# Delta-rule attention with an MoE layer on one core: GpSimd's clamp, sign and scaling in other two-operation forms, all signs on GpSimd, new planner costs and ranks

## The chip, the cores and the metric

One NeuronCore of a Trainium2 chip. The time is device microseconds from start to end of one execution. A run of the kernel before gives 619.16 to 619.97 us.

## The reference

Delta-rule attention over 4 batches, 8 heads, 768 steps, head size 48, and behind it a layer of 384 to 2048 to 384 whose weights come in as 64-bit floats.

```python
def _attn_ref(q, k, v, beta):
    k_n = k / (np.linalg.norm(k, axis=-1, keepdims=True) + 1e-06)
    for t in range(S):
        kt, vt, bt = (k_n[:, :, t], v[:, :, t], beta[:, :, t, None])
        y[:, :, t] = np.einsum('bhd,bhde->bhe', q[:, :, t], state)
        v_old = np.einsum('bhde,bhd->bhe', state, kt)
        state = state + bt[:, :, :, None] * np.einsum('bhd,bhe->bhde', kt, vt - v_old)

def _moe_ref(x, w_in, w_out):          # x: 3072 x 384, from y
    h = x @ w_in
    sp = np.where(h > 20.0, h, np.log1p(np.exp(np.minimum(h, 20.0))))
    return ((h * np.tanh(sp)) @ w_out).astype(np.float32)
```

## The kernel before

**Chunks.** The 768 steps are cut into 12 chunks of 64. Two chunks make a group. `early(g)` does a group's part that needs no state: it loads and transposes the keys (`kt`, L531), multiplies them with themselves (`pg`, L547/L553), masks the products (L562, L567, L576), turns them (L591), and solves a triangular system row by row on VectorE (L673/L674, transposes L687 to L698). For groups 0 and 1 the solve is split in halves, which `merge(n)` joins with two sets of small products, `ma` (L718) and `mb` (L730). Then per chunk come the stages `s_a`, `s_b` (`ta`, `tb`), `s_gq`, `s_z` and `s_y`, all issued from L753; the last one yields the new state and the chunk's 384 x 256 input `x` to the layer (L1080, L1081).

**The layer.** `moe(n)` works on chunk n in eight units. A unit is an up group of 18 matmuls (`h`, L1108), Mish, a cast and a difference (L1124 to L1126), and a down group of 12 matmuls (`acc`, L1118). So the whole kernel has 96 up and 96 down groups.

**The weights.** The 64-bit weights are 28 parts, three `i` parts (128x512) and four `o` parts (128x384) for each quarter of the layer. `convert(k)` turns part k into a pair of 32-bit matrices: ScalarE scales the upper words (L429), a clamp (L443) on GpSimd or VectorE, a sign (L440 on GpSimd, L438 on VectorE), two joins on VectorE (L447) which shift in the lower bits, a negated rounding on ScalarE (L459), and the remainder, on VectorE (L470) for the first 13 parts and over TensorE (L464, L466, L468) from part 13. Clamps are on GpSimd for all parts but part 6; signs are on VectorE for 14 of the 28 parts. Units 0 and 1 of a chunk need quarter 0 of the `i` parts, units 2 and 3 quarter 1, and so on.

**The order.** Nothing runs in program order. Each step is an `op(engine, took, rank, ...)`, and `Plan.run` replays all engines with the durations `took`, takes at each moment the ready step of least rank, and so writes the order of every engine's queue once, when the kernel is built. Ranks are in units of chunks: `moe(n)` has n to n+1 (its differences n + fp/8 + 0.1, its down groups n + (fp + LAG)/8), `convert(k)` has `CV0 + CV1 k/28`, and `early(1)` has `E1 + E1S x`, where x is 0 at the loads of the keys, 0.02 to 0.2 at the transposes, 0.3 to 0.9 in the solve and 0.94 at the merge. Stages of chunk 1 take `c1`, those of later chunks `cc`.

**Loads.** All go through SyncE's queue but some at the start. `EW` is the part from which the loads of weights wait for the group products of chunk 1; `HELD` is a part whose load waits for the first `ma`; `PACE` is how many parts a load may be ahead of the scaling of the parts before it; `KW` picks the weight loads that the first keys and values follow. `BURN` counts tiny matmuls (16x16) between chunk 0's stages. `scale_v` scales a chunk's values by the keys' norms, on ScalarE to chunk 3 and on GpSimd from chunk 4 (L912, eight instructions of 48 columns).

Of the kernel before, what the change touches and what calls it, by code (L numbers as in the profile page):

```python
# [13 lines left out]
ALU = mybir.AluOpType  # L14
# [54 lines left out]
class Plan:  # L69
# [18 lines left out]
    def op(self, engine, took, prio, fn, *after, bufs=(), kb=0, words=0):  # L88
        o = Op(engine, took, prio, fn, after, [b for b in bufs if b is not None])
        o.kb, o.words = kb, words  # L90
        for b in o.bufs:
            b.ops.append(o)
        self.ops.append(o)
        return o
# [127 lines left out]
def kernel(  # L222
# [181 lines left out]
    def convert(k, got, loads):  # L404
        kind, i = parts[k]
        n = 512 if kind == "i" else DM
        u = n / 512.0
        prio = PRIO_CV(k)
        tag = TEMPS[k] if k < len(TEMPS) else ("t0", "t1", "w", "w", "s0", "s1")[(k - len(TEMPS)) % 6]
        if tag in ("t0", "t1"):  # L410
            tmp = Buf(tag, lambda: solved().rearrange("p a b -> p (a b)")[:, 512 * int(tag[1]):512 * int(tag[1]) + 512])
            held = [tmp, solved]
        elif tag in ("s0", "s1"):
            base = spare[int(tag[1])]
            tmp = Buf(tag, lambda: base()[:, 0:512])
            held = [tmp, base]
        else:
            tmp = buf(tag, [P, 512], f"m{kind}{i}")
            held = [tmp]

        def a():
            return tmp()[:, :n]

        def words():
            return raw[kind, i].rearrange("p (a b) -> p a b", b=2)


        def scaled():
            marks[copied[k]] = nc.scalar.activation(a(), words()[:, :, 1].bitcast(F32), AF.Copy, scale=2.0 ** -112).ins  # L429

        copied[k] = o = op("ACT", 0.16 + 0.51 * u, prio, scaled, got, bufs=held)
        if EW < k < len(parts) - PACE:
            loads[k + PACE].after.append(o)

        def sign(engine):
            s = words()[:, :, 1].bitcast(F32)
            if engine == "DVE":
                nc.vector.tensor_scalar(words()[:, :, 1], words()[:, :, 1], -2 ** 31, None, op0=ALU.bitwise_and)  # L438
            else:
                nc.gpsimd.tensor_scalar(s, a(), 0.0, None, op0=ALU.mult)  # L440

        def clamp(engine):
            engine.tensor_scalar(a(), a(), -F64_MOST * 2.0 ** -112, F64_MOST * 2.0 ** -112, op0=ALU.max, op1=ALU.min)  # L443

        def join(x, n, f):
            ai = a().bitcast(I32)
            return nc.vector.scalar_tensor_tensor(ai, *((ai, n, x) if f == ALU.logical_shift_left else (x, n, ai)), op0=f, op1=ALU.bitwise_or).ins  # L447

        o = op("POOL", 0.25 + 1.72 * u, prio, lambda: clamp(nc.gpsimd), o, bufs=held) if k in CLAMP_POOL else \
            op("DVE", 0.14 + 0.39 * u, prio, lambda: clamp(nc.vector), o, bufs=held)  # L450

        e = "DVE" if k in SIGN_DVE else "POOL"
        o = op(e, 0.13 + 0.38 * u if e == "DVE" else 0.43 + 1.12 * u, prio, lambda: sign(e), o, bufs=held)
        o = op("DVE", 0.06 + 0.8 * u, prio, lambda: join(words()[:, :, 1], 3, ALU.logical_shift_left), o, bufs=held)
        o = op("DVE", 0.06 + 0.8 * u, prio, lambda: join(words()[:, :, 0], 29, ALU.logical_shift_right), o, bufs=held)

        def first():
            w = wt[kind, i] = cp.tile([P, 2, n], F32R, tag=f"w{kind}{i}", name=f"w{kind}{i}")
            nc.scalar.mul(out=w[:, 0], in_=a(), mul=-1.0)  # L459

        hi = op("ACT", 0.16 + 0.47 * u, prio, first, o, bufs=held)
        if k in LO_PE:
            ps = buf(f"acc{k % 2}" if k < 6 else "ps", [P, 512], f"lo{kind}{i}")
            p1 = op("PE", 0.05 + 0.5 * u, prio, lambda: nc.tensor.matmul(ps()[:, :n], ident, a(), start=True, stop=False),  # L464
                    o, eyer, bufs=[*held, ps], words=4)
            p2 = op("PE", 0.03 + 0.22 * u, prio, lambda: nc.tensor.matmul(  # L466
                ps()[:, :n], identr, wt[kind, i][:, 0], start=False, stop=True), p1, hi, bufs=[ps], words=2)
            return op("ACT", 0.12 + 0.48 * u, prio, lambda: nc.scalar.mul(  # L468
                out=wt[kind, i][:, 1], in_=ps()[:, :n], mul=-1.0), p2, bufs=[ps])
        return op("DVE", 0.1 + 0.58 * u, prio, lambda: nc.vector.scalar_tensor_tensor(  # L470
            wt[kind, i][:, 1], a(), -1.0, wt[kind, i][:, 0], op0=ALU.mult, op1=ALU.subtract), hi, bufs=held)
# [50 lines left out]
    def early(g, at, gate=None):  # L522
# [3 lines left out]
        for t2 in range(2):  # L526
# [45 lines left out]
            if g:  # L572

                def first_block(hh, t2=t2, am=am):
                    r = slice(64 * hh, 64 * hh + 32)
                    nc.gpsimd.affine_select(out=dt()[r, t2], in_=am()[r], pattern=[[0, NP], [1, 32]], compare_op=ALU.is_ge, fill=0.0,  # L576
                                            base=0, channel_multiplier=-1)

                last = last_s["at", n]
                outs += [op("POOL", 1.37, at(0.17 + 0.03 * t2), lambda hh=hh, f=first_block: f(hh), last, *outs[-2:], made, bufs=[am, dt])  # L580
                         for hh in range(2)]
                last_s["first", n] = outs[-2:]
        gr = buf("gt", [P, 33, 32], f"gt{g}")
# [67 lines left out]

        if g < ROOTS:
            o = op("DVE", 0.38, at(0.25), norms, o, last_s.get("root"), bufs=[gr])
            o = op("ACT", 1.7 if g else 0.25, at(0.25), guess, o)
            last_s.setdefault("guess", o)
            o = op("DVE", 1.45, at(0.25), root, o)
        else:
            o = op("DVE", 3.9, at(0.25), lambda: (norms(), steps(), root()), o, last_s.get("root"), bufs=[gr])
        o = op("DVE", 0.93 if split else 1.45, at(0.26), scale, o, cut, *(betas if g == 0 else ()), bufs=[gr])
        nes[g] = ne  # L660
        ned[g] = last_s["root"] = op("DVE", 0.25, at(0.27), turned, o, last_s.get("turned"), bufs=[bp, ne])
# [29 lines left out]
        if split:  # L691
            ym = buf(*(("gt", [P, 33, 32]) if g else ("g", [P, 32, 32])), f"ym{g}")
            c = op("POOL", 0.6, at(0.9), lambda: nc.gpsimd.memset(ym()[:, :32, 16:], 0.0), u if g else cleared_rest, bufs=[ym])
            last_s["ym"] = c
            for t2 in range(2):
                merge(2 * g + t2, lambda x, t2=t2: at(0.94 + x) + 0.3 * t2 if g or not t2 else XA - 0.25 + x, u, c, o, dt, tu, ym, tn)
        else:
            tnd[2 * g] = tnd[2 * g + 1] = op("DVE", 2.24, at(0.97), lambda: nc.vector.transpose(  # L698
                tn().rearrange("p a b j -> p j (a b)"), gt().rearrange("p i j -> p j i")), o, bufs=[gr, tn])
            for t2 in range(2):  # L700
                ttd[2 * g + t2] = op("POOL", 1.42, at(0.98), lambda t2=t2: move_diagonal(t2), o)
# [198 lines left out]
    def scale_v(n, h, prio, *after):  # L900
        vt, ne = vts[n, h], nes[n // 2]
        n16 = NP * (n % 2) + PB * h
        if n <= 3:
            def scaled():
                for p in range(PB):
                    nc.scalar.mul(out=vt()[:, p, :], in_=vt()[:, p, :], mul=ne()[:, n16 + p:n16 + p + 1])

            vdn[n, h] = op("ACT", 1.9, prio, scaled, ned[n // 2], *after, bufs=[vt.base, ne])
            return
        def scaled():  # L910
            for p in range(PB):
                nc.gpsimd.tensor_scalar(vt()[:, p, :], vt()[:, p, :], ne()[:, n16 + p:n16 + p + 1], None, op0=ALU.mult)  # L912

        vdn[n, h] = op("POOL", 3.4, prio, scaled, ned[n // 2], *after, bufs=[vt.base, ne])

    def turn_q(n, h, prio, got):
        def turn():
# [219 lines left out]
                   bufs=[o], kb=0.3)  # L1137


    SOON, SOON1, E1, EG, ES, LATE1, LATE = -0.099, 2.914, 0.577, -0.653, 1.745, 0.496, 0.249  # L1140
    E1S, LAG, PRIO_XT, CV0, CV1, G1A, XA, GQ2 = 0.074, 3.993, 0, -0.2, 0.877, 1.076, 0.45, 1.157
    LO_PE = range(13, 28)
    HELD, MASKS, ROOTS = 5, 1, 2
    plan.MARGIN = 1
    KW, EW, BURN, TQ, PACE = 2, 0, 84, 2, 4
    plan.TOGETHER = 0.003
    CLAMP_POOL = [k for k in range(len(parts)) if k < 6 or k >= 7 and k % 4 < 4]
    SIGN_DVE = [k for k in range(len(parts)) if k % 4 >= 2]
    TEMPS = ("g", "g", "e", "e", "w", "w", "s0", "s1")

    def PRIO_CV(k):
# [38 lines left out]
    for h in range(2):  # L1190
        issue(0.01 + 0.05 * h, s_y(0, h, y=False))

    cc = [x - SOON for x in (0.05, 0.28, 0.5, 0.72)]
    c1 = [x - SOON1 for x in (0.3, 0.45, 0.68, 0.82)]
    nxt = {1: prep(1, -0.2)}

    def ready(n, h, prio):
# [79 lines left out]
```

## Time and profile before

| | |
|---|---|
| timed runs | 619.16, 619.7 and 619.97 us, median 619.7 |
| span of the profiled execution, its own time | 621.0 us |
| mean granted TensorE clock | 0.956 |
| busy, TensorE matmul / VectorE / ScalarE / GpSimd | 584.7 / 438.9 / 282.0 / 174.3 us |

The profiled execution has no time besides its span, so 1.3 us lie between it and the median of the runs. A share over the whole span mixes two stages: a start, in which weights are converted and the first chunks' states are worked out, and a long stretch in which TensorE has units of the layer to do all the time.

### The profile page before, as it was taken

Reading aid. Unit: us, or ns where it says so; the run is one execution under the profiler, and the core shown is the slowest. Engines: PE = TensorE matmul, PEld = TensorE weight load, DVE = VectorE, ACT = ScalarE, POOL = GpSimd, SP = SyncE. Lnnn points to the kernel's source line nnn. Section 1 sums busy time; section 2 is a strip of 40 time slices with the busy share of each in tenths; the row PEclk is TensorE's granted clock in tenths of the full one; section 3 lists DMA queues with packets and bytes.
Section 4 is the critical chain, followed back from the end, with each engine's and each line's share of the span. In section 5 each row is a group of like instructions: output and inputs, shape, how many; then the busy total and the mean of one; then the engine's idle time right before and its main releaser. Section 6 shows DMA issues by size and latency. Waiting matters only on the chain.

```text
span 621.0 us, 23486 instructions
## 1 busy us (share of the span) xinstructions
PE 584.7 (94%) x10264; PEld 543.1 (87%) x10264; DVE 438.9 (71%) x955; ACT 282.0 (45%) x631; POOL 174.3 (28%) x259
## 2 busy tenths in 40 slices
PE   7657999998899999999999999999999999999997
PEld 4346877897889999999999899999899999999996
DVE  4869899987168999379897579895789893631110
ACT  1838787574344333544324534335433335343321
POOL 6469799211000442013051014131104420000000
PEclk9657899997699999999999999999999999999999
DMA  7958655341025123243114333114041220110001
GB/s 115 225 146 244 150 169 115 54 52 29 4 33 95 18 41 52 29 67 67 30 23 70 42 56 53 33 26 67 17 81 25 41 49 6 29 28 1 6 22 27
DMA packets 156264, 37.81 MB, mean 61 GB/s; under 512 B 149504, under 2 KB 152576, under 8 KB 156160
## 3 DMA queue, kind: packets, MB, share of 16 engines
q1 hardware_dynamic: 151040, 35.80, 29.4%
q8 instruction: 81, 1.33, 1.0%
q10 hardware_dynamic: 5120, 0.49, 0.6%
q14 instruction: 23, 0.19, 0.1%
HBM read 31.56 MB, written 4.72 MB: 58 GB/s over the span
## 4 chain that ended last, share of the span: by engine, by line
PE 78%; POOL 9%; DVE 5%; issue 3%; ACT 2%; DMA 1%; POOLq 0%; DVEq 0%
PE acc L1118 32%; PE h L1108 31%; PE py L753 3%; PE gq L753 3%; PE pz L753 2%; POOL mi L443 2%; PE pg L547 2%; PE ps L753 2%; POOL spare L443 2%; POOL ro L440 1%; POOL solved L443 1%; PE tb L753 1%; POOL ri L440 1%; PE ta L753 1%; PE warm L491 1%
## 5 line engine op out<-in xcount | busy, mean ns | idle before, releaser
L1108 PE MATMUL h<-x,wi 128*128 128x256 f32 x1728 | 226.3, 287 | 1.3 <-issue 0.6
L1118 PE MATMUL acc<-wo,g 128*128 128x384 f32 x1152 | 224.7, 345 | 1.8 <-issue 1.7
L1108 PEld LDWEIGHTS h<-x,wi 128*128 128x128 f32 x1728 | 218.2, 192 | 4.4 <-issue 0.8
L1118 PEld LDWEIGHTS acc<-wo,g 128*128 128x128 f32 x1152 | 201.8, 191 | 7.9 <-issue 4.0
L1126 DVE TENSOR_TENSOR g<-e,g 128x512 fp32r<-128x512 f32 x96 | 69.5, 729 | 93.3 <-ACT g L1125 81.3
L1124 ACT ACTIVATE e<-h 128x512 f32<-128x512 f32 x96 | 57.4, 598 | 126.0 <-PE h L1108 71.6
L1125 ACT CAST g<-e 128x512 fp32r<-128x512 f32 x96 | 59.5, 620 | 65.7 <-PE acc L1118 64.3
L912 POOL TENSOR_SCALAR vt<-vt,ne 128x48 f32<-128x48 f32 x128 | 57.5, 475 | 65.9 <-DMA vt<-in_v_dram 49.3
L674 DVE TENSOR_TENSOR gt<-gt,pr 128x84 f32<-128x84 f32 (+14 forms) x148 | 48.9, 330 | 5.1
L673 DVE TENSOR_TENSOR pr<-gt 128x84 f32<-128x84 f32 (+14 forms) x148 | 47.4, 321 | 3.4
L576 POOL TENSOR_SCALAR_AFFINE_SELECT d<-at 32x512 f32<-32x512 f32 x20 | 14.4, 720 | 101.1 <-ACT at L567 100.3
L777 ACT COPY xx<-pz 64x192 f32<-64x192 f32 x92 | 28.9, 314 | 22.2 <-PE pz L753 20.7
L970 DVE TENSOR_TENSOR xx<-gq,amask 64x256 f32<-64x256 f32 x88 | 37.1, 422 | 1.6
L706 POOL COPY tt<-tt 32x512 f32<-32x512 f32 x24 | 17.4, 725 | 71.3 <-DVE tt L689 49.2
L963 DVE TENSOR_TENSOR vt<-vt,gq 64x192 f32<-64x192 f32 (+1 forms) x66 | 23.3, 353 | 19.0 <-PE gq L753 18.1
L753 PE MATMUL gq<-xx,kt 64*64 64x112 f32 (+1 forms) x768 | 30.6, 264 | 2.5 <-ACT xx L938 2.5
L1067 DVE TENSOR_TENSOR xx<-xx,ps 48x192 f32<-48x192 f32 x80 | 28.2, 352 | 3.2 <-PE ps L753 1.6
L921 DVE STREAM_TRANSPOSE xx<-qsrc 64x512 f32<-64x512 f32 x40 | 28.2, 706 | 1.1
L753 PEld LDWEIGHTS py<-xx 128*32 128x32 f32 (+1 forms) x1536 | 23.5, 111 | 5.7 <-issue 3.6
L753 PE MATMUL py<-xx 128*32 128x64 f32 (+1 forms) x1536 | 27.8, 227 | 0.7 <-ACT xx L777 0.4
L753 PE MATMUL pz<-vt,tt 64*64 64x48 f32 x768 | 27.8, 225 | 0.6 <-ACT tt L777 0.6
L753 PEld LDWEIGHTS pz<-vt,tt 64*64 64x64 f32 x768 | 22.7, 140 | 5.3 <-issue 2.1
(146 smaller groups left out, 611.4 us busy)
## 6 DMA issues: line engine op xcount, KB each, us to landing
ri<-in_moe_w_in_dram SPq DMA_DIRECT2D x12, 512.0 KB, 5.2
ro<-in_moe_w_out_dram SPq DMA_DIRECT2D x16, 384.0 KB, 4.4
vt<-in_v_dram SPq DMA_DIRECT2D x24, 192.0 KB, 4.4
xx<-in_k_dram SPq DMA_DIRECT2D x48, 96.0 KB, 3.1
out_dram<-o SPq DMA_DIRECT2D x48, 96.0 KB, 2.2
ksrc<-in_k_dram SPq DMA_DIRECT2D x44, 64.0 KB, 3.0
qsrc<-in_q_dram SPq DMA_DIRECT2D x40, 64.0 KB, 2.5
ksrc<-in_k_dram SPq DMA_DIRECT2D x44, 32.0 KB, 2.6
```

The costliest lines, as they stand in the source:

```text
L443: engine.tensor_scalar(a(), a(), -F64_MOST * 2.0 ** -112, F64_MOST * 2.0 ** -112, op0=ALU.max, op1=ALU.min)
L673: nc.vector.tensor_tensor(out=pv, in0=nj, in1=xj, op=ALU.mult)
L674: return nc.vector.tensor_tensor(out=below, in0=below, in1=pv, op=ALU.add).ins
L753: last = nc.tensor.matmul(*a, **flags)
L777: (nc.scalar.copy if e == "ACT" else nc.vector.tensor_copy)(out=a, in_=b)
L912: nc.gpsimd.tensor_scalar(vt()[:, p, :], vt()[:, p, :], ne()[:, n16 + p:n16 + p + 1], None, op0=ALU.mult)
L970: nc.vector.tensor_tensor(out=x[r, p4, hh, Q0:K0], in0=pg[h4]()[i, :, d:], in1=bcast_mid(amask[i], 4), op=ALU.mult)
L1108: nc.tensor.matmul(h()[:, f2, :], wt["i", f * P // WI * NCH + c][:, i2, f0:f0 + P], x[:, c, :], start=(i == 0), stop=(i == 3 * NCH - 1))
L1118: nc.tensor.matmul(acc[t]()[:, :DM], gg()[:, a, f2, ts_], wt["o", f][:, i2, :], start=(f == 0 and i == 0), stop=(f == NF - 1 and i == 2))
L1124: m = op("ACT", 0.58, prio + 0.1, lambda e=e, h=h: nc.scalar.activation(e(), h(), AF.Mish, scale=-1.0), m, bufs=[h, e])
L1125: m = op("ACT", 0.58, prio + 0.1, lambda e=e, gg=gg: nc.scalar.copy(out=gg()[:, 0], in_=e()), m, bufs=[e, gg])
L1126: m = op("DVE", 0.72, prio + 0.1 - PRIO_XT * (n == 1), lambda e=e, gg=gg: nc.vector.tensor_tensor(out=gg()[:, 1], in0=e(), in1=gg()[:, 0], ...
```

## The change

The clamp becomes min first, then max; the sign, a multiplication by 0, gets a second multiplication by 1; so does the scaling of V. All 28 signs go to GpSimd. The planner's durations for these and for some other steps are set anew. The loads' numbers (`HELD`, `KW`, `EW`, `PACE`), `BURN` and all ranks are changed. They compute the same values.

```diff
--- before.py
+++ after.py
@@ -437,22 +437,22 @@
             if engine == "DVE":
                 nc.vector.tensor_scalar(words()[:, :, 1], words()[:, :, 1], -2 ** 31, None, op0=ALU.bitwise_and)
             else:
-                nc.gpsimd.tensor_scalar(s, a(), 0.0, None, op0=ALU.mult)
+                nc.gpsimd.tensor_scalar(s, a(), 0.0, 1.0, op0=ALU.mult, op1=ALU.mult)
 
         def clamp(engine):
-            engine.tensor_scalar(a(), a(), -F64_MOST * 2.0 ** -112, F64_MOST * 2.0 ** -112, op0=ALU.max, op1=ALU.min)
+            engine.tensor_scalar(a(), a(), F64_MOST * 2.0 ** -112, -F64_MOST * 2.0 ** -112, op0=ALU.min, op1=ALU.max)
 
         def join(x, n, f):
             ai = a().bitcast(I32)
             return nc.vector.scalar_tensor_tensor(ai, *((ai, n, x) if f == ALU.logical_shift_left else (x, n, ai)), op0=f, op1=ALU.bitwise_or).ins
 
-        o = op("POOL", 0.25 + 1.72 * u, prio, lambda: clamp(nc.gpsimd), o, bufs=held) if k in CLAMP_POOL else \
+        o = op("POOL", 0.33 + 0.45 * u, prio, lambda: clamp(nc.gpsimd), o, bufs=held) if k in CLAMP_POOL else \
             op("DVE", 0.14 + 0.39 * u, prio, lambda: clamp(nc.vector), o, bufs=held)
 
         e = "DVE" if k in SIGN_DVE else "POOL"
-        o = op(e, 0.13 + 0.38 * u if e == "DVE" else 0.43 + 1.12 * u, prio, lambda: sign(e), o, bufs=held)
-        o = op("DVE", 0.06 + 0.8 * u, prio, lambda: join(words()[:, :, 1], 3, ALU.logical_shift_left), o, bufs=held)
-        o = op("DVE", 0.06 + 0.8 * u, prio, lambda: join(words()[:, :, 0], 29, ALU.logical_shift_right), o, bufs=held)
+        o = op(e, 0.13 + 0.38 * u if e == "DVE" else 0.3 + 0.45 * u, prio, lambda: sign(e), o, bufs=held)
+        o = op("DVE", 0.05 + 0.65 * u, prio, lambda: join(words()[:, :, 1], 3, ALU.logical_shift_left), o, bufs=held)
+        o = op("DVE", 0.05 + 0.65 * u, prio, lambda: join(words()[:, :, 0], 29, ALU.logical_shift_right), o, bufs=held)
 
         def first():
             w = wt[kind, i] = cp.tile([P, 2, n], F32R, tag=f"w{kind}{i}", name=f"w{kind}{i}")
@@ -577,7 +577,7 @@
                                             base=0, channel_multiplier=-1)
 
                 last = last_s["at", n]
-                outs += [op("POOL", 1.37, at(0.17 + 0.03 * t2), lambda hh=hh, f=first_block: f(hh), last, *outs[-2:], made, bufs=[am, dt])
+                outs += [op("POOL", 0.78, at(0.17 + 0.03 * t2), lambda hh=hh, f=first_block: f(hh), last, *outs[-2:], made, bufs=[am, dt])
                          for hh in range(2)]
                 last_s["first", n] = outs[-2:]
         gr = buf("gt", [P, 33, 32], f"gt{g}")
@@ -651,11 +651,11 @@
 
         if g < ROOTS:
             o = op("DVE", 0.38, at(0.25), norms, o, last_s.get("root"), bufs=[gr])
-            o = op("ACT", 1.7 if g else 0.25, at(0.25), guess, o)
+            o = op("ACT", 2.7 if g else 1.4, at(0.25), guess, o)
             last_s.setdefault("guess", o)
             o = op("DVE", 1.45, at(0.25), root, o)
         else:
-            o = op("DVE", 3.9, at(0.25), lambda: (norms(), steps(), root()), o, last_s.get("root"), bufs=[gr])
+            o = op("DVE", 3.65, at(0.25), lambda: (norms(), steps(), root()), o, last_s.get("root"), bufs=[gr])
         o = op("DVE", 0.93 if split else 1.45, at(0.26), scale, o, cut, *(betas if g == 0 else ()), bufs=[gr])
         nes[g] = ne
         ned[g] = last_s["root"] = op("DVE", 0.25, at(0.27), turned, o, last_s.get("turned"), bufs=[bp, ne])
@@ -695,7 +695,7 @@
             for t2 in range(2):
                 merge(2 * g + t2, lambda x, t2=t2: at(0.94 + x) + 0.3 * t2 if g or not t2 else XA - 0.25 + x, u, c, o, dt, tu, ym, tn)
         else:
-            tnd[2 * g] = tnd[2 * g + 1] = op("DVE", 2.24, at(0.97), lambda: nc.vector.transpose(
+            tnd[2 * g] = tnd[2 * g + 1] = op("DVE", 2.1, at(0.97), lambda: nc.vector.transpose(
                 tn().rearrange("p a b j -> p j (a b)"), gt().rearrange("p i j -> p j i")), o, bufs=[gr, tn])
             for t2 in range(2):
                 ttd[2 * g + t2] = op("POOL", 1.42, at(0.98), lambda t2=t2: move_diagonal(t2), o)
@@ -909,9 +909,9 @@
             return
         def scaled():
             for p in range(PB):
-                nc.gpsimd.tensor_scalar(vt()[:, p, :], vt()[:, p, :], ne()[:, n16 + p:n16 + p + 1], None, op0=ALU.mult)
-
-        vdn[n, h] = op("POOL", 3.4, prio, scaled, ned[n // 2], *after, bufs=[vt.base, ne])
+                nc.gpsimd.tensor_scalar(vt()[:, p, :], vt()[:, p, :], ne()[:, n16 + p:n16 + p + 1], 1.0, op0=ALU.mult, op1=ALU.mult)
+
+        vdn[n, h] = op("POOL", 3.3, prio, scaled, ned[n // 2], *after, bufs=[vt.base, ne])
 
     def turn_q(n, h, prio, got):
         def turn():
@@ -1137,15 +1137,16 @@
                    bufs=[o], kb=0.3)
 
 
-    SOON, SOON1, E1, EG, ES, LATE1, LATE = -0.099, 2.914, 0.577, -0.653, 1.745, 0.496, 0.249
-    E1S, LAG, PRIO_XT, CV0, CV1, G1A, XA, GQ2 = 0.074, 3.993, 0, -0.2, 0.877, 1.076, 0.45, 1.157
+    SOON, SOON1, E1, EG, ES, LATE1, LATE = 0.043, 13.71, 0.365, -0.298, 2.321, 0.932, 0.634
+    E1S, LAG, PRIO_XT, CV0, CV1, G1A, XA, GQ2 = 0.774, 3.149, 0, 0.135, 0.479, 0.665, -1.246, 1.55
+    CC, C1 = (0.281, -4.756, 0.363, 0.824), (0.842, -0.794, -1.026, 0.245)
     LO_PE = range(13, 28)
-    HELD, MASKS, ROOTS = 5, 1, 2
+    HELD, MASKS, ROOTS = 6, 1, 2
     plan.MARGIN = 1
-    KW, EW, BURN, TQ, PACE = 2, 0, 84, 2, 4
+    KW, EW, BURN, TQ, PACE = 0, 2, 100, 2, 6
     plan.TOGETHER = 0.003
     CLAMP_POOL = [k for k in range(len(parts)) if k < 6 or k >= 7 and k % 4 < 4]
-    SIGN_DVE = [k for k in range(len(parts)) if k % 4 >= 2]
+    SIGN_DVE = []
     TEMPS = ("g", "g", "e", "e", "w", "w", "s0", "s1")
 
     def PRIO_CV(k):
@@ -1190,8 +1191,8 @@
     for h in range(2):
         issue(0.01 + 0.05 * h, s_y(0, h, y=False))
 
-    cc = [x - SOON for x in (0.05, 0.28, 0.5, 0.72)]
-    c1 = [x - SOON1 for x in (0.3, 0.45, 0.68, 0.82)]
+    cc = [x - SOON for x in CC]
+    c1 = [x - SOON1 for x in C1]
     nxt = {1: prep(1, -0.2)}
 
     def ready(n, h, prio):
```

## Rows read from the trace of the kernel before

**Rows 1.** The page's span.
```profile
span 621.0 us, 23486 instructions
```

**Rows 2.** Windows, all engines: busy us and instructions, granted clock, DMA.
```profile
56.00:80.00 24.00, 19.08 (x445) 17.34 (x441) 21.42 (x37) 19.35 (x51) 19.25 (x15) 0.93 0.64 175
80.00:110.00 30.00, 30.00 (x347) 23.43 (x346) 27.81 (x45) 25.14 (x56) 29.50 (x19) 1.00 0.54 135
110.00:150.00 40.00, 36.64 (x730) 33.96 (x729) 35.36 (x84) 23.70 (x65) 5.58 (x9) 0.95 0.33 49
150.00:194.50 44.50, 41.09 (x1097) 37.88 (x1096) 21.57 (x41) 17.78 (x43) 5.51 (x8) 0.85 0.17 28
194.50:608.00 413.50, 410.87 (x6547) 395.45 (x6546) 292.73 (x668) 166.12 (x349) 77.83 (x160) 1.00 0.23 39
```

**Rows 3.** Windows of L1108 alone, from 56 to 194.5 us.
```profile
56.00:194.50 138.50, 41.31 (x288) 39.05 (x289) 0.93 0.38 83
```

**Rows 4.** Chain that ended last, around 85 us: start, us, what.
```profile
83.79 1.64 POOL ri L440
85.43 1.45 POOL mo L443
```

**Rows 5.** Windows over the whole span: L443, then L440, then L447.
```profile
0.00:621.00 621.00, 0.77 (x1) 48.59 (x27) 0.96 0.31 61
...
0.00:621.00 621.00, 19.91 (x14) 0.96 0.31 61
...
0.00:621.00 621.00, 39.81 (x56) 0.96 0.31 61
```

**Rows 6.** Groups by form: the two signs on VectorE.
```profile
L438 DVE TENSOR_SCALAR ro<-ro 128x384 int32<-128x384 int32 x8 | 4.0, 503 | 0.0
L438 DVE TENSOR_SCALAR ri<-ri 128x512 int32<-128x512 int32 x6 | 3.9, 655 | 0.0
```

**Rows 7.** Instructions of a line: ns min/median/max; clamp, sign, copy, selection, V.
```profile
L443 POOL TENSOR_SCALAR mi<-mi x6: 1926/2060/2246, 27.7 to 100.0; 128x512 f32<-128x512 f32 x6
L443 POOL TENSOR_SCALAR mo<-mo x6: 1488/1578/1663, 44.1 to 85.4; 128x384 f32<-128x384 f32 x6
...
L440 POOL TENSOR_SCALAR ri<-mi x3: 1522/1642/1752, 29.7 to 83.8; 128x512 f32<-128x512 f32 x3
...
L706 POOL COPY tt<-tt x24: 601/610/1072, 40.0 to 512.7; 32x512 f32<-32x512 f32 x24
...
L912 POOL TENSOR_SCALAR vt<-vt,ne x128: 393/404/1284, 202.9 to 497.4; 128x48 f32<-128x48 f32 x128
```

**Rows 8.** Joins on VectorE: ns min/median/max.
```profile
L447 DVE SCALAR_TENSOR_TENSOR mi<-ri,mi x6: 692/836/998, 33.6 to 104.2; 128x512 int32<-128x512 int32 x6
L447 DVE SCALAR_TENSOR_TENSOR mo<-mo,ro x6: 550/558/852, 46.7 to 88.6; 128x384 int32<-128x384 int32 x6
```

**Rows 9.** Timeline from 31 us, GpSimd and VectorE: start, us.
```profile
31.45 1.93 POOL L443 TENSOR_SCALAR mi<-mi 128x512 f32<-128x512 f32 x1
32.91 0.70 DVE L447 SCALAR_TENSOR_TENSOR mi<-mi,ri 128x512 int32<-128x512 int32 x1
33.46 1.52 POOL L440 TENSOR_SCALAR ri<-mi 128x512 f32<-128x512 f32 x1
33.64 0.98 DVE L447 SCALAR_TENSOR_TENSOR mi<-ri,mi 128x512 int32<-128x512 int32 x1
```

**Rows 10.** Timeline: last join, solve of group 1, and TensorE behind it.
```profile
118.16 0.51 DVE L447 SCALAR_TENSOR_TENSOR solved<-ro,solved 128x384 int32<-128x384 int32 x1
...
126.74 2.04 DVE L591 STREAM_TRANSPOSE gt<-d 128x1024 f32<-128x1024 f32 x1
...
157.17 4.21 PE L1108 MATMUL h<-x,wi 128*128 128x256 f32 x18
...
194.56 4.44 PE L1108 MATMUL h<-x,wi 128*128 128x256 f32 x36
```

**Rows 11.** The page's DMA issues: one part of the input weights, KB, us to landing.
```profile
ri<-in_moe_w_in_dram SPq DMA_DIRECT2D x12, 512.0 KB, 5.2
```

## The prediction

> **What bounds the kernel now.** The execution to be predicted against has a span of 621.0 us [rows 1]. The windows come first [rows 2]. From 194.5 to 608 us TensorE is busy 410.87 of 413.5 us at full clock, so there nothing but its own work counts: whatever is done earlier before 194.5 us comes off the end. The question is what makes the layer's units of chunk 2 begin only at 194.56 us [rows 10]. Before that moment exactly 288 up matmuls, the 16 groups of chunks 0 and 1, have run [rows 3]. From 56 to 194.5 us TensorE stood idle for 4.92 + 0 + 3.36 + 3.41 = 11.7 us, and ran part of the time at its lower level of 1.2 GHz, granted 0.93, 1.00, 0.95 and 0.85 of 2.4 GHz on the mean, which is worth 24 x 0.07 + 40 x 0.05 + 44.5 x 0.15 = 10.4 us. So 22.1 us are the most that this stretch can give back.
>
> Then I ask which engine holds chunk 2 back. Between 80 and 110 us GpSimd is busy 29.50 of 30 us and VectorE 27.81 [rows 2], and the chain that ended last runs there from clamp to sign to clamp on GpSimd [rows 4]. That is the conversion of the weights. The last join ends at 118.7 us; VectorE begins the big transpose ahead of group 1's solve at 126.74 us, and 68 us later the units of chunk 2 begin [rows 10]. VectorE has to do both, the joins and the solve, and is nearly full: this is the second bound, right behind GpSimd.
>
> **What the change costs and saves, part by part.**
>
> *Clamp and sign on GpSimd.* Now they take 48.59 and 19.91 us, 68.5 together, 27 clamps and 14 signs [rows 5]. The trace has no min-then-max clamp and no sign with a second operation. The bounds are the same operations as they are, 2.06 and 1.64 us for 512 columns [rows 7], and a plain copy of 512 columns on 32 partitions, 0.61 us [rows 7]. The planner's new figures, 0.33 + 0.45 = 0.78 and 0.30 + 0.45 = 0.75 us, are an input of the diff and no measurement, but they lie close to the copy, and I take them: 12 x 0.78 + 15 x 0.67 = 19.4 us for the clamps, 12 x 0.75 + 16 x 0.64 = 19.2 us for 28 signs, 38.6 us together. GpSimd loses 29.9 us and ceases to be the bound; the next that is late is VectorE, and the gain is what VectorE saves, not 29.9.
>
> The clamp's row grows by (2.060 - 1.578) / 128 = 3.8 ns per column [rows 7]. The Trainium skill (GPSIMD Engine Reference, 3.1 Elementwise) has a loop of up to two operations on one input bound by the ports at 1.03 cycles per element, whatever the operations are. An estimate from that page at its 1.2 GHz is 0.86 ns per column for old and new form alike, so by it the form brings nothing; the measured 3.8 ns differs from it, and a mechanism by which the form does not matter stands among the rivals below.
>
> *Signs off VectorE.* Fourteen go, 4.0 + 3.9 = 7.9 us [rows 6]. Nothing new waits: the sign followed the clamp before, and on GpSimd only the next clamp is queued behind it; the joins wait for it as they did.
>
> *Joins.* They take 39.81 us now, 56 of them [rows 5]. One beside a clamp took 0.70 us, the next, beside a sign, 0.98 us [rows 9]; for 384 columns the ends are 0.55 and 0.85 [rows 8]. So some GpSimd work slows VectorE, and the new forms are of a quicker kind. Lower end: 24 x 0.70 + 32 x 0.54 = 34.0 us. Upper end, all joins slowed: 24 x 0.98 + 32 x 0.85 = 50.8 us. If the slow ones are as many as GpSimd is busy between the first clamp at 27.7 [rows 7] and the last join, 38.6 of 91 us, they take 34.0 + 0.42 x 16.8 = 41.1 us. I go halfway between 34.0 and 41.1, 37.5: 2.3 us saved, bounds 5.8 saved and 11.0 lost.
>
> *VectorE's gaps.* From 56 to 110 us it idled 2.58 + 2.19 = 4.8 us [rows 2], some of it for GpSimd. With GpSimd ahead I take half of it, 2.4, bounds 0 and 4.8.
>
> *Scaling of V.* 0.404 us now, 3.3 / 8 = 0.41 by the planner. It runs from 202.9 us [rows 7], where GpSimd is busy 77.83 of 413.5 us [rows 2]: nothing, in either direction, as long as that room is there; without cover, a change by the whole 0.4 us would cost or give 128 x 0.4 = 51 us of GpSimd, which still fits into its idle 336.
>
> *Loads, BURN, the planner's other costs.* Two parts of the weights now go out ahead of the queries and values on SyncE's queue, and later parts may be two further ahead. One part lands 5.2 us after its issue [rows 11]. From 5.2 us lost, if chunk 0 waits for it, to 2.4 us gained, if VectorE's gaps close because parts are there sooner (counted above); I take 0. Sixteen more tiny matmuls at the planner's 0.008 us are 0.1 us, in a place where TensorE waits anyway. The other costs move no instruction by themselves.
>
> *Ranks.* All queues get another order, which can't be read off the rows. What they can win is the rest of the 22.1 us above; what they can lose is priced as a rival. I take 0.
>
> *Sum.* VectorE is done with the weights 7.9 + 2.3 + 2.4 = 12.6 us sooner, the solve of group 1 and chunk 2's units begin as much sooner, and TensorE has 22.1 us of slack there to fit the same work: 621.0 - 12.6 = 608.4 us of span. The median of the runs shown lies 1.3 us below the span, so 607.1 us. The bounds of the terms give 7.9 - 11.0 = -3.1 (3.1 us slower) to 7.9 + 5.8 + 4.8 = 18.5 us saved.
>
> **The rivals.**
>
> *All slack goes.* If the new ranks also interleave chunk 2's stages so that TensorE neither idles nor falls to 1.2 GHz, 22.1 us and the 2.6 us idle of the long stretch are won: 621.0 - 24.7 - 1.3 = 595.0 us. For it: between 150 and 194.5 us VectorE is busy only 21.57 of 44.5 us [rows 2], so the wait there is order, not work. Against it: an up group at 157.17 us took 4.21 us, where two take 4.44 us at full clock [rows 10], and chunk 2's stages are a chain with a wait at every step.
>
> *Contention eats it.* All joins are slowed, VectorE saves nothing (-3.1 + 2.4): 621.0 + 0.7 - 1.3 = 620.4 us. For it: 0.98 beside 0.70 us [rows 9]. Against it: GpSimd will be busy less than half of that time. The Trainium skill (SBUF — State Buffer, two separate sides) lets a VectorE operation with two inputs and a GpSimd operation exclude each other for the whole instruction. The join of 0.70 us ran inside a clamp of 1.93 us without such a wait, the one of 0.98 us was stretched by less than the sign beside it; by that rule contention would cost more, and the trace bears it out only in part.
>
> *Slower: chunk 2 falls behind the layer.* E1S goes from 0.074 to 0.774, so the merge of chunk 2 has rank 0.365 + 0.774 x 0.94 = 1.09 instead of 0.65, that of chunk 3 about 1.39 instead of 0.95. Down groups of chunk 0 have fp/8 + 0.39 now: six go ahead of the first merge instead of two, and some four up groups of chunk 1 ahead of the second. Eight groups at 4.44 / 2 = 2.2 us [rows 10] are 17.8 us, against 12.6 won: chunk 2 comes 5 us later, and these units are then missing as cover in the following stretch, where one took 4.21 us; I put another 5 us on that: 621.0 + 10 - 1.3 = 629.7 us. It decides from six groups on (6 x 2.2 = 13). Against it: E1 itself falls from 0.577 to 0.365, so the group's loads and products come earlier.
>
> *The form does not matter.* Then GpSimd has 28 signs at 19.91 / 14 = 1.42 us, 19.9 us more, and is the bound alone: 621.0 + 19.9 - 1.3 = 639.6 us. Against it: at 3.8 ns per column the old clamp is far from the copy's 0.61 / 512 = 1.2 ns, so its form costs something that another need not.
>
> **How the numbers follow.** Forecast 607.1 us, chance 0.56, with a range of its own from 600 to 614; all slack goes 0.14; contention 0.10; chunk 2 behind 0.13; form 0.07. A change of 0.2%, 1.2 us, is about what can be told from none. Faster: 0.55 + 0.14 + 0.03 of contention = 0.72. Same: 0.05 of contention and 0.01 = 0.06. Slower: 0.02 + 0.13 + 0.07 = 0.22. The range reaches from below the all-slack case, 593, to 624, which holds the contention case and leaves out the form's case and most of the slower one.
>
> **What would show it.** Right: clamps and signs near 0.75 us, no sign on VectorE, GpSimd half idle between 80 and 110 us and gone from the chain there, the last join near 106 us, chunk 2's units from 182 us, the long stretch as full as before. Wrong: clamps near 2 us; joins near 0.98 us throughout; the last join early but chunk 2 as late as before, which would put the bound in the order of merges and stages; or new gaps of TensorE behind 200 us.

## The result, and the profile after

The changed kernel takes 613.34 us (median of nine runs, 610.89 to 617.99) against 619.7 (618.01 to 620.04) for the kernel before: ratio 0.9895, 95% interval 0.9865 to 0.9926. It is faster, by half of the 12.6 us forecast. The profiled execution took 614.27 us, 1.8 us more than its span. In the runs that were timed for the experiments, those of the kernel before included, the difference is 1.7 to 1.9 us as well, so the profiled execution of before, with its span of 621.0 us, probably was a long one, near 622.7. By spans the gain is 8.5 us, by medians 6.4; so some 2 us of what the two traces differ by below probably belong to the execution and not to the kernel.

The page of after: the span, and the engines' busy time, share and instructions.

```profile
span 612.5 us, 23525 instructions
PE 579.4 (95%) x10280; PEld 538.5 (88%) x10280; DVE 430.8 (70%) x941; ACT 281.0 (46%) x631; POOL 143.3 (23%) x273
...
PE 85%; DVE 6%; issue 3%; POOL 2%; DMA 2%; ACT 1%; ACTq 0%; POOLq 0%; DVEq 0%
```

TensorE's matmuls take 5.3 us less than before (584.7 us in the table ahead), and it idles 33.1 instead of 36.3 us: 5.3 + 3.2 = 8.5. Most of the 5.3 us is the clock: granted 0.962 against 0.956 on the mean, which is worth 621.0 x 0.044 - 612.5 x 0.038 = 4 us by an estimate. The last line is the chain that ended last, by engine; GpSimd has 2% of it, after 9% before.

The windows of after, to be read against [rows 2]: busy us of PE, PEld, DVE, ACT, POOL, then granted clock and DMA.

```profile
56.00:80.00 24.00, 20.01 (x585) 17.57 (x574) 23.68 (x37) 21.94 (x56) 15.24 (x20) 0.90 0.84 176
80.00:110.00 30.00, 28.98 (x378) 23.28 (x377) 23.20 (x38) 21.98 (x50) 17.74 (x23) 1.00 0.63 144
110.00:150.00 40.00, 39.93 (x880) 36.92 (x881) 32.92 (x79) 26.20 (x66) 4.76 (x9) 1.00 0.23 36
150.00:194.50 44.50, 41.52 (x972) 38.71 (x966) 27.90 (x67) 19.19 (x45) 8.12 (x19) 0.96 0.22 39
194.50:608.00 413.50, 411.86 (x6546) 395.52 (x6544) 282.77 (x640) 163.93 (x349) 68.93 (x148) 1.00 0.22 38
```

From 80 to 110 us GpSimd fell from 29.50 to 17.74 us, and from 110 to 194.5 TensorE is fuller and at a better clock. VectorE was not full behind GpSimd: 23.20 of 30 us, less than before. The long stretch was nearly full and still is.

What the changed instructions take: the sums over the span for L443 (the first number is VectorE's one clamp), L440 and L447, as [rows 5].

```profile
0.00:612.00 612.00, 0.35 (x1) 21.26 (x27) 0.96 0.32 62
...
0.00:612.00 612.00, 20.84 (x28) 0.96 0.32 62
...
0.00:612.00 612.00, 40.45 (x56) 0.96 0.32 62
```

And ns min/median/max of single ones, as [rows 7]: clamp, sign, and the scaling of V.

```profile
L443 POOL TENSOR_SCALAR mi<-mi x6: 614/772/1122, 17.8 to 98.7; 128x512 f32<-128x512 f32 x6
L443 POOL TENSOR_SCALAR mo<-mo x6: 508/808/956, 33.3 to 79.6; 128x384 f32<-128x384 f32 x6
...
L440 POOL TENSOR_SCALAR ri<-mi x6: 652/819/1173, 18.5 to 99.4; 128x512 f32<-128x512 f32 x6
...
L912 POOL TENSOR_SCALAR vt<-vt,ne x128: 298/354/992, 190.6 to 483.3; 128x48 f32<-128x48 f32 x128
```

A clamp of 512 columns went from 2.06 to 0.77 us and a sign from 1.64 to 0.82, by the medians of these rows. The quickest ones take 0.61 and 0.65, near the plain copy in [rows 7]. Joins did not shorten: 40.45 against 39.81 us.

Three rows of after show how it went on, as [rows 10]: last join, big transpose ahead of group 1's solve, main run of chunk 2's units (one matmul of theirs ran at 184.14 us).

```profile
113.29 0.56 DVE L447 SCALAR_TENSOR_TENSOR solved<-ro,solved 128x384 int32<-128x384 int32 x1
118.39 2.03 DVE L591 STREAM_TRANSPOSE gt<-d 128x1024 f32<-128x1024 f32 x1 [0.52 <-PE loo L464]
...
187.42 7.93 PE L1108 MATMUL h<-x,wi 128*128 128x256 f32 x53 [2.89 <-DVE x L1081]
```

The last join is 4.9 us sooner, the solve 8.4, chunk 2 7.1, the end 8.5. The 2.89 us in brackets is a new wait, which e5 takes up.

**Where the solve's 8.4 us come from.** Windows of VectorE alone, from zero to L591, of before and then of after.

```profile
0.00:126.74 126.74, 104.33 (x193) 0.87 0.64 150
```

```profile
0.00:118.39 118.39, 93.95 (x170) 0.83 0.71 161
```

VectorE did 10.38 us less before the solve and idled 2.03 us more (24.44 against 22.41). Of the 10.38, 7.9 are the signs; joins cost 0.6 more; the remaining 3.1 is other work, now ordered behind the solve: differences of the layer (8 before it in the kernel before, 5 now), transposes of queries and the like. So at the solve: 7.9 - 0.6 - 2.0 + 3.1 = 8.4.

VectorE's waits for a sign ahead of the solve, us in total, times, longest; first before, then after.

```profile
DVE mi L447 <- POOL ri L440: 0.4, 1, 0.4
DVE spare L447 <- POOL ro L440: 0.4, 2, 0.2
DVE mo L447 <- POOL ro L440: 0.3, 1, 0.3
...
DVE solved L447 <- POOL ro L440: 0.2, 1, 0.2
```

```profile
DVE spare L447 <- POOL ro L440: 3.3, 2, 2.2
...
DVE mi L447 <- POOL ri L440: 1.6, 1, 1.6
DVE solved L447 <- POOL ro L440: 1.5, 2, 1.0
...
DVE solved L447 <- POOL ri L440: 0.6, 1, 0.6
```

In the kernel before, VectorE lost 1.3 us in all to a GpSimd that was busy 29.50 of 30 us: its order already had other work in those places. With clamps and signs two to three times as quick it loses 7.0.

### The profile page after: what moved, and what is told of

It reads as the page before. It is cut to its first block, busy times and chain, and to the rows that moved or that the text cites. A ratio compares the mean times of both kernels' runs of the same rounds, so it can differ in the third digit from the quotient of the medians.

```text
span 612.5 us, 23525 instructions
## 1 busy us (share of the span) xinstructions
PE 579.4 (95%) x10280; PEld 538.5 (88%) x10280; DVE 430.8 (70%) x941; ACT 281.0 (46%) x631; POOL 143.3 (23%) x273
## 4 chain that ended last, share of the span: by engine, by line
PE 85%; DVE 6%; issue 3%; POOL 2%; DMA 2%; ACT 1%; ACTq 0%; POOLq 0%; DVEq 0%
PE h L1108 34%; PE acc L1118 33%; PE py L753 4%; PE gq L753 3%; PE pz L753 2%; PE pg L547 2%; PE ps L753 2%; PE tb L753 1%; PE ta L753 1%; PE loo L464 1%; DMA ri<-in_moe_w_in_dram 1%; DVE gt L674 1%; DVE pr L673 1%; DMA ro<-in_moe_w_out_dram 1%; DVE spare L447 1%
## 5 line engine op out<-in xcount | busy, mean ns | idle before, releaser
L1108 PE MATMUL h<-x,wi 128*128 128x256 f32 x1728 | 224.3, 285 | 3.0 <-DVE x L1081 2.9
L1108 PEld LDWEIGHTS h<-x,wi 128*128 128x128 f32 x1728 | 215.7, 190 | 6.6 <-DVE x L1081 3.1
L1118 PE MATMUL acc<-wo,g 128*128 128x384 f32 x1152 | 220.6, 341 | 0.0
L1118 PEld LDWEIGHTS acc<-wo,g 128*128 128x128 f32 x1152 | 198.7, 188 | 3.4 <-issue 0.2
L1126 DVE TENSOR_TENSOR g<-e,g 128x512 fp32r<-128x512 f32 x96 | 67.2, 703 | 113.9 <-ACT g L1125 113.7
L912 POOL TENSOR_SCALAR vt<-vt,ne 128x48 f32<-128x48 f32 x128 | 52.2, 433 | 64.9 <-DMA vt<-in_v_dram 32.8
L673 DVE TENSOR_TENSOR pr<-gt 128x84 f32<-128x84 f32 (+14 forms) x148 | 47.4, 320 | 3.0
```

The costliest lines, as they stand in the source:

```text
L673: nc.vector.tensor_tensor(out=pv, in0=nj, in1=xj, op=ALU.mult)
L1108: nc.tensor.matmul(h()[:, f2, :], wt["i", f * P // WI * NCH + c][:, i2, f0:f0 + P], x[:, c, :], start=(i == 0), stop=(i == 3 * NCH - 1))
L1118: nc.tensor.matmul(acc[t]()[:, :DM], gg()[:, a, f2, ts_], wt["o", f][:, i2, :], start=(f == 0 and i == 0), stop=(f == NF - 1 and i == 2))
L1126: m = op("DVE", 0.72, prio + 0.1 - PRIO_XT * (n == 1), lambda e=e, gg=gg: nc.vector.tensor_tensor(out=gg()[:, 1], in0=e(), in1=gg()[:, 0], ...
```

## The experiments

Each was timed in five rounds beside the kernel before, whose medians were 619.67 (e1 to e4), 619.52 (e5 to e8) and 618.44 us (e9 to e11). Ratios are to it, with their 95% intervals.

**e1: the three forms alone, every engine's order as before.**

```diff
 kernel before
-  sign  a, 0.0, None, op0=mult            +  a, 0.0, 1.0, op0=mult, op1=mult
-  clamp op0=max, op1=min                  +  op0=min, op1=max
-  V     ne, None, op0=mult                +  ne, 1.0, op0=mult, op1=mult
```

> The kernel before with nothing but the three new forms (clamp min then max, sign and scaling of V with a second multiplication); every engine's order is that of before. If GpSimd's time in the conversion is what held the first chunks back, the 68.5 us of clamps and signs fall to about 35 and the time falls by 10 us or more, to 609 or less. If VectorE is the next bound right behind it, as predicted, the signs still on VectorE and joins no shorter than before leave 2 to 6 us: 614 to 618. If the new order alone made the gain, nothing: 619 to 620.

Measured: 619.42 us, ratio 0.9996 [0.9976, 1.0016]. GpSimd's busy time fell from 174.3 to 127.0 us, and its share of the chain that ended last from 9% to 1%; the time did not move. VectorE's window to the solve in e1, the sums of clamps and of joins in e1, and the transpose ahead of the solve:

```profile
0.00:126.50 126.50, 103.74 (x193) 0.87 0.65 150
```

```profile
0.00:620.00 620.00, 0.82 (x1) 18.57 (x27) 0.96 0.31 61
...
0.00:620.00 620.00, 37.17 (x56) 0.96 0.31 61
```

```profile
126.50 2.03 DVE L591 STREAM_TRANSPOSE gt<-d 128x1024 f32<-128x1024 f32 x1
```

Under this order GpSimd at 29.50 of 30 us was no bound. VectorE's joins took 37.17 us, 2.6 less, yet VectorE was busy only 0.6 less before the solve, among other things since group 0's own solve beside the clamps got slower (14 products of L673 took 4.81 instead of 4.07 us), and its idle time did not shrink.

**e2: the change with the three old forms, order as after.** The edit is e1's, reversed, in the changed kernel.

> The changed kernel with the three old forms, its order on every engine kept. If the quick forms are needed for this order, GpSimd has 49 us of clamps and 40 us of signs, is busy without a break to beyond 115 us, and the time rises by 12 us or more, to 625 to 640. If the order carries the gain, it stays at 612 to 615.

Measured: 632.82 us, ratio 1.0224 [1.0195, 1.0253]. Here the forms are worth 19.5 us. VectorE's window to the solve, its waits for signs, and the sum of its joins:

```profile
0.00:138.02 138.02, 94.87 (x169) 0.79 0.60 138
```

```profile
DVE spare L447 <- POOL ro L440: 8.9, 6, 2.9
DVE mi L447 <- POOL ri L440: 7.2, 4, 3.6
...
DVE solved L447 <- POOL ri L440: 4.5, 4, 2.0
DVE solved L447 <- POOL ro L440: 3.7, 3, 1.3
...
DVE mo L447 <- POOL ro L440: 3.0, 3, 1.1
```

```profile
0.00:630.00 630.00, 43.56 (x56) 0.95 0.30 60
```

VectorE has about as little work as after (94.87 against 93.95 us), but idles 43.2 us, over 27 of them for signs. So the same forms are worth nothing in the old order and 19.5 us in the new, which leans on them and gives all signs to GpSimd. The joins, in the same order, are 3.1 us longer beside the old forms (43.56 against 40.45), as they were 2.6 us longer in the order of before (39.81 against 37.17 in e1).

**e3: the loads of before.**

```diff
 changed kernel
-HELD 6, KW 0, EW 2
+HELD 5, KW 2, EW 0
```

> The changed kernel with the numbers of the loads as before (HELD 5, KW 2, EW 0, PACE 6 kept, BURN kept), planned anew. Theory: two weight loads and a conversion ahead of chunk 0's queries made the first up group start 9 us later (65.7 instead of 56.5 us) and cost time to the end; then the first group starts by 60 us and the time is 607 to 610. Rival: the late start is hidden, since chunk 2's units wait for the solve of group 1 on VectorE anyway; then 612 to 616.

Measured: 615.0 us, ratio 0.9915 [0.9892, 0.9938], its interval overlapping that of the changed kernel; the solve at 118.50, chunk 2 at 187.09 us. The loads' numbers are worth nothing that shows. `PACE` and `BURN` stayed as changed, so those two were not tried by themselves.

**e4: the 14 signs back on VectorE.**

```diff
 changed kernel
-SIGN_DVE = []
+SIGN_DVE = [k for k in range(len(parts)) if k % 4 >= 2]
```

> The changed kernel with the 14 signs of before back on VectorE, planned anew. If VectorE bounds the conversion, 5 to 8 us more VectorE work comes back as 3 to 8 us: 616 to 621. If VectorE has room there (23.2 of 30 us busy from 80 to 110 us), 612 to 615.

Measured: 617.05 us, ratio 0.9951 [0.9927, 0.9974]. The signs' move is worth 3.7 us by medians, not 7.9, and even that is loose: the changed kernel run once more (e9) has the ratio 0.9913, 2.4 us from this one, and the intervals overlap. VectorE's joins in e4:

```profile
0.00:615.00 615.00, 38.08 (x56) 0.96 0.31 61
```

VectorE took 7.23 us for the signs, but its joins 2.4 us less than in the changed kernel, 38.08 instead of 40.45. It looks as if signs on GpSimd lengthen the joins that they spare VectorE the time for, though e4 has an order of its own. Ahead of the solve, other work was 1.7 us less and idle time 1.1 less (23.32 against 24.44), so that the solve starts at 120.41 us, only 2.0 later.

**e5: VectorE's block ahead of chunk 2 cut in three.** A step of 3.65 us (norms, steps and root of the next group) stood ahead of the addition that gives chunk 2's `x`, and TensorE waited 2.89 us for it.

```diff
 changed kernel
-o = op("DVE", 3.65, at(0.25), lambda: (norms(), steps(), root()), o, ...)
+o = op("DVE", 0.25, at(0.25), norms, o, ...)
+o = op("DVE", 1.95, at(0.25), steps, o)
+o = op("DVE", 1.45, at(0.25), root, o)
```

> The changed kernel with the 3.65 us block of norms, root steps and root of a group (from group 2 on) handed to the planner as three steps of 0.25, 1.95 and 1.45 us, so that the difference which TensorE waits 2.89 us for at 187 us can go ahead. If that wait and the half clock behind it set the end, 608 to 611. If the planner's new order gives it back elsewhere, 612 to 616.

Measured: 611.03 us, ratio 0.9863 [0.9833, 0.9893]; against the changed kernel not told apart by itself (the intervals overlap). The wait fell to 1.4 us (lines are two higher in this kernel), and another one, 2.7 us in the changed kernel, was 3.3 here:

```profile
187.32 10.19 PE L1110 MATMUL h<-x,wi 128*128 128x256 f32 x71 [1.44 <-DVE x L1083]
```

```profile
PE ps L755 <- issue: 3.3, 1, 3.3
```

**e6: forms, signs and durations of after, all ranks and loads of before.**

```diff
 kernel before
+the three forms, SIGN_DVE = [], the planner's durations of the change
```

> The changed kernel with the ranks and the numbers of the loads of before; forms, all signs on GpSimd and the planner's new durations stay. Theory now: the quick forms pay only through an order that is planned with their durations, so a new plan with the old ranks gets part of the gain: 614 to 617, the last join before 116 us. If the ranks themselves make the gain, no change: 619 to 622.

Measured: 625.39 us, ratio 1.0090 [1.0060, 1.0119]: slower than before. The solve starts at 122.23 us, 4.5 sooner than before, and chunk 2's units run from 193.38; behind 150 us TensorE idles more than before, and the long stretch is a little less full (410.87 us before):

```profile
150.00:194.50 44.50, 38.85 (x976) 36.12 (x971) 24.68 (x56) 17.42 (x42) 4.20 (x7) 0.91 0.21 38
194.50:608.00 413.50, 409.33 (x6534) 393.85 (x6534) 285.12 (x650) 165.58 (x348) 70.47 (x159) 1.00 0.23 38
```

**e7: the change, planned with the old durations.** The chip runs the same steps; only the numbers from which the order is worked out are those of before.

```diff
 changed kernel
-clamp 0.33 + 0.45 u, sign 0.3 + 0.45 u, join 0.05 + 0.65 u, norms 3.65, ...
+clamp 0.25 + 1.72 u, sign 0.43 + 1.12 u, join 0.06 + 0.8 u, norms 3.9, ...
```

> The changed kernel, planned with the durations of before (clamp 1.97, sign 1.55 us and so on); the instructions and ranks are the changed ones. If the durations are what places the joins and the solve, the order is as if GpSimd were slow and the gain is lost: 618 to 626. If the ranks decide, 612 to 616.

Measured: 623.5 us, ratio 1.0061 [1.0034, 1.0088], slower than before. Its profiled execution was its fastest (618.46 us), so its trace shows the loss only in part; the last join ends at 120.5, and the solve starts at 123.34 us.

**e8: group 1's work at a lower rank.**

```diff
 changed kernel
-E1 = 0.365
+E1 = 0.1
```

> The changed kernel with E1 0.1 in place of 0.365, so that group 1's transposes and solve come ahead of more conversions. If the end follows the start of that solve (118.4 us) one to one, some 3 to 6 us less: 607 to 611. If the conversions that it displaces starve the layer's units on TensorE, 613 to 620.

Measured: 622.03 us, ratio 1.0050 [1.0024, 1.0075], slower. The solve came no sooner (118.99 us) and chunk 2's units 75.7 us behind it, where the changed kernel has 69.0. From 110 to 150 us TensorE, full in the changed kernel, idles 4.5 us at a lower clock:

```profile
110.00:150.00 40.00, 35.48 (x771) 32.21 (x771) 32.91 (x79) 23.78 (x63) 5.68 (x9) 0.91 0.17 28
```

**e9, e10, e11: the changed kernel once more; with e5's cut and e3's loads; with the conversion's old ranks.** All on one chip.

```diff
 changed kernel (e9 as it is)
 e10: +the three steps of e5, +HELD 5, KW 2, EW 0
 e11: -CV0, CV1 = 0.135, 0.479   +CV0, CV1 = -0.2, 0.877
```

> The changed kernel itself, to be compared with the next two on one chip. Both theories: 612 to 615 us, a ratio of 0.985 to 0.993 to the kernel before.

> The changed kernel with the 3.65 us step of norms, steps and root cut in three and the loads' numbers of before. If the cut takes away VectorE's block ahead of chunk 2 whatever the order around it (first theory), it wins as much as the wait that it removes, 1.5 to 2.9 us: 610.5 to 612. If every edit of a step draws a new order whose quality is chance (second theory), it lies anywhere between 609 and 620, with no relation to the wait of 2.89 us.

> The changed kernel with the conversion's two rank constants of before alone (start -0.2 for 0.135, slope 0.877 for 0.479). If the gain sits in the place of the conversion among the other work, the whole gain goes: 619 us or more, with the last join several us later than 113.3 or the solve behind 118.4. If it sits in the ranks of the group's solve and the stages, it stays within 2 us of the changed kernel, 611 to 615.

Measured: e9 613.41 us, 0.9913 [0.9887, 0.9939]; e10 610.85 us, 0.9879 [0.9854, 0.9904]; e11 615.31 us, 0.9943 [0.9921, 0.9965]. e10's median is 2.6 us below the changed kernel's, inside the 1.5 to 2.9 us that its wait could give, and it is the fastest of all that ran; but the intervals overlap, so it beats the kernel before for certain and the changed one only probably. Its wait is 1.4 us, and the solve came sooner too, so the cut's own share is not told apart from the new order's:

```profile
183.44 10.20 PE L1110 MATMUL h<-x,wi 128*128 128x256 f32 x71 [1.43 <-DVE x L1083]
```

```profile
115.97 2.05 DVE L591 STREAM_TRANSPOSE gt<-d 128x1024 f32<-128x1024 f32 x1 [1.28 <-PE loo L464]
```

e11 keeps two thirds of the gain, within 2 us of e9, against the theory that the gain sits in the place of the conversion alone.

**The ladder.** Before 619.7; forms alone 619.4; forms, signs and durations under old ranks 625.4; new ranks with old durations 623.5; everything 613.3; everything but the forms 632.8. None of the parts that were tried alone gives the gain. The order that gives it was worked out from short durations, and it needs the forms that make them true (e2). That their being true is what matters is not shown: the new ranks and durations came together, e6 and e7 each part them, and an order that differs by one rank can lose nearly as much (e8, 8.7 us). The new ranks by themselves, with the forms, signs and durations of before, were not run.

## Why the prediction came out as it did

The direction was right and the time lay in the range; the forecast itself was 6.2 us too low. That it came so near is in part luck. The sum prices the forms and the signs and puts the ranks at nothing; with the old ranks and loads the other edits made the kernel 5.7 us slower (e6), and only the ranks that it had put at nothing turned that into a gain. By its own steps:

- *Clamp and sign on GpSimd*, 38.6 us: 21.26 + 20.84 = 42.1. The copy was the right row to price the new forms by. At their quickest (0.61 and 0.51, 0.65 and 0.53 us) all of them would take about 31 us; the rest is probably contention. The form-does-not-matter rival is out: with the old forms the time is 632.8 us, as e2 shows. The new clamp's row grows by (614 - 508) / 128 = 0.83 ns per column. The estimate of 0.86 from the Trainium skill (GPSIMD Engine Reference, 3.1 Elementwise) agrees with the new form; the old one, of as many operations, took 3.8, and there the measurement decides.
- *"GpSimd ... ceases to be the bound"*: **this failed as a reading of before.** GpSimd was busy, and it was in the chain that ended last, but it did not bind: VectorE waited 1.3 us for it in all, and e1 gave nothing, with GpSimd all but gone from the chain. The row to ask was VectorE's waits for GpSimd, not GpSimd's busy share or its place in the chain. The sentence behind it, that the gain is what VectorE saves, held up to the solve (the 8.4 us above) and not for the kernel, where e6 has a solve 4.5 us sooner and a longer time.
- *Signs off VectorE*, 7.9 us: right for VectorE's own instructions, mis-sized for the time. e4 measured 3.7 us, loosely, with 2.4 us coming back as longer joins and 1.1 us as idle time of VectorE ahead of the solve.
- *Joins*, 2.3 us saved: they cost 0.6 more. Two effects that the term did not part nearly cancel: the quick forms shorten the joins by 2.6 us (e1) or 3.1 (e2 to after), about as the term has it, and the 14 signs that came to GpSimd seem to lengthen them by 2.4 (e4 to after). The contention rival was right in kind and wrong in price. (The term's upper end adds up to 50.7, not 50.8 us.)
- *VectorE's gaps*, 2.4 us saved: lost instead. From 56 to 110 us VectorE idled 0.32 + 6.80 = 7.1 us, 2.3 more than before, and up to the solve 2.0 more, for signs and for data, as the rows above show.
- *V and loads at nothing*: right. V's instruction fell from 404 to 354 ns behind a full TensorE, and e3 moved nothing.
- *"The other costs move no instruction by themselves"*: wrong. They are what the order is worked out from; the changed kernel planned with all the old durations takes 623.5 us (e7), 10 more.
- *Ranks at nothing*: **this failed too.** With the old ranks the other edits cost 5.7 to 5.9 us (e6), so the new ranks, with the loads' numbers that e3 found worth nothing, bring 12.1 us on top (625.4 to 613.3). Of the 9.1 us between the spans of these two traces, 3.8 lie ahead of the solve (122.23 to 118.39), 2.1 between it and chunk 2's main run (71.2 to 69.0 us), and 3.1 behind that.
- *"Whatever is done earlier ... comes off the end"*: held from chunk 2 on: from the start of its main run to the end of the span it is 426.4 us before, 425.1 after, and 423.5 to 428.2 in all thirteen traces. The link ahead of it, a sooner solve and so a sooner chunk 2, does not always hold: these two are 67.2 to 69.9 us apart in eleven traces, 71.2 in e6 and 75.7 in e8, whose solves, 4.5 and 7.8 us sooner than before's, bought nothing. Their main runs:

```profile
193.38 5.93 PE L1108 MATMUL h<-x,wi 128*128 128x256 f32 x35 [1.87 <-DVE x L1081]
```

```profile
194.70 8.08 PE L1108 MATMUL h<-x,wi 128*128 128x256 f32 x53 [2.89 <-DVE x L1081]
```

- *From span to median*, -1.3 us: for the changed kernel it is +0.8, which is 2.1 us of the 6.2. The other 4.1 are the sum's: 8.5 us by spans instead of 12.6, with the last join done at 113.9 us and not near 106, and chunk 2's main run from 187 us and not 182.
- *All slack goes*: no. From 56 to 194.5 us TensorE still idles 8.1 us, of 11.7, and the new wait of 2.89 us is among them.
- *Slower rival, chunk 2 behind the layer*: the late merge did not bring it. But its mechanism, an order in which chunk 2 comes late, is what e8 made with another rank.

What stays open: which rank brings the 12.1 us, and whether the new ranks would gain without the forms. e8 and e11 moved one or two ranks and lost 8.7 and 1.9 us; each such edit draws a new order of all engines, so losses of single edits do not add up. A rival stands with that: ranks and durations may simply be a pair that draws a good order, and another pair might do as well.

## What to carry to other kernels

Before calling a full engine the bound, ask who waited for it and how long: 1.3 us of waits told, for the order as it was, what forms that took 47 us off GpSimd were worth. Where an order is worked out ahead, a quicker instruction is worth what the order makes of it: the same forms were worth 0 us in one and 19.5 us in the other, and working the order out again was not enough either, since under the old ranks it lost 5.7 us. Price work moved between two engines that slow each other by what both then take, not by what the first one saves.

## What the runs showed of the hardware

- The order of two comparisons sets GpSimd's time: max then min took 1.93 us at the least for 512 columns, min then max 0.61. A multiplication with a second one took 0.65 us, by itself 1.52. For eight instructions on 48 columns it was 298 against 393 ns each.
- Beside quick GpSimd forms the joins take less in all, not more: under the same order 37.17 us beside quick and 39.81 beside slow ones (e1, before), 40.45 and 43.56 (after, e2). But a quick clamp and a join nearly exclude each other. In after, from 19 us:

```profile
19.23 0.69 DVE L447 SCALAR_TENSOR_TENSOR mi<-mi,ri 128x512 int32<-128x512 int32 x1 [1.56 <-POOL ri L440]
19.28 1.12 POOL L443 TENSOR_SCALAR mi<-mi 128x512 f32<-128x512 f32 x1
19.96 0.98 DVE L447 SCALAR_TENSOR_TENSOR mi<-ri,mi 128x512 int32<-128x512 int32 x1
```

  The clamp takes 0.61 us at the least and took 1.12, the second join 0.98 instead of 0.69. That is near what two instructions that exclude each other would do, the clamp from the end of the first join, 19.92 + 0.61 = 20.53 us, where it ended at 20.40, and the second join from there. A slow clamp leaves room. The join of [rows 9] lay beside its clamp for only 0.47 of its 0.70 us, which is less than the prediction reads there, but another one of before lay wholly inside:

```profile
57.26 2.25 POOL L443 TENSOR_SCALAR solved<-solved 128x512 f32<-128x512 f32 x1
...
58.58 0.69 DVE L447 SCALAR_TENSOR_TENSOR spare<-spare,ri 128x512 int32<-128x512 int32 x1
```

  The Trainium skill (SBUF — State Buffer, SBUF: two separate sides) has such an exclusion for the whole instruction; the quick forms agree with it here, the slow clamp of before, with a join at full speed inside it, does not. In e2 a join that began 0.08 us behind a slow clamp of 1.93 us, at 109.46 us, took 1.07 us, and the next one, inside the same clamp, 0.69: there only the first part of the clamp seems to hold a join back.
- Behind the same wait of TensorE for chunk 2's `x`, 2.9 us long, the same 53 up matmuls took 6.55 us at a granted clock of 1.00 (e11, 2.4 GHz throughout), 7.93 at 0.81 (after) and 9.05 at 0.69 (e7, both partly at 1.2 GHz). What decides between them no run shows; these three executions differ by up to 2.5 us there.
